# Sliding-window attention with sinks and a highway layer: scores in key halves, with bias and sinks' values issued among them

## The chip, the cores and the metric

The kernel runs on one core of a Trainium2 chip. The metric is device time in microseconds (us) of one execution, the median of several runs; lower is better. The core has a matrix engine (TensorE, called PE in the profile; its weight loads are the row PEld), a vector engine (VectorE, DVE), a scalar engine (ScalarE, ACT), a general engine (GpSimd, POOL) and SyncE (SP), which here only issues DMAs. TensorE writes its results to PSUM, which ACT and DVE read.

## The reference

Four batches, eight heads, 768 positions, head size 64. Each query sees the four first keys (the sinks) and the 128 newest keys up to itself. The result goes through a highway layer of width 512.

```python
keep = is_sink | in_window          # pos < 4, or 0 <= query - key < 128
scores = np.where(keep, scale * q @ k.T, -1e9)
a = softmax(scores)
x = (a @ v)                         # to (3072, 512), the heads side by side
H = np.maximum(x @ w_h, 0.0)
T = 1.0 / (1.0 + np.exp(-(x @ w_t + b_t)))
return T * H + (1.0 - T) * x
```

## The kernel before

The 4 x 768 positions are cut into N = 24 blocks of 128, six to a batch (block n is block c = n % 6 of batch n // 6). The loop runs over n from 0 to 25 as a pipeline: in turn n the kernel makes the scores of the keys of block n, the attention values of block n-1 (n1) and the highway layer of block n-2 (nb). The order of the instructions on each engine is that in which the code issues them; `_keep_traced_order` forbids any other.

**Scores (L264 to L283).** The keys of block n are seen by the queries of blocks n and n+1, 256 queries in all (128 in the last block of a batch). Keys stand on the 128 output rows, queries on the columns. Heads lie in four groups of 32 partitions (g = 0 to 3, two heads hg in each, and the 64 numbers of a head in two halves e), so every product contracts over 32 partitions and uses one of four row groups of the matrix array. The masks come first: for each x (own queries, next block's queries) and g one matmul of 32 rows, 128 columns of weights and 256 moving columns (L271) adds a very negative number where the key isn't in the window. Then 16 matmuls of the same shape add the scores (L278). `expo` (L326, ACT) takes the exponential of all of it out of PSUM.

**Starts (L304 to L318).** Between the scores and the values stand the first products of two accumulations, in the same 32-row shape: the bias of the gate (L310, one matmul of 512 columns into `ps_z`) and the sinks' share of the values (L316, two matmuls of 260 columns into `ps_av`, both in row group j = t-2, with t the block's place in its batch; the first two blocks of a batch have none). The bias stands in another row group than the sinks.

**Values and the highway layer.** 16 matmuls of 128 x 128 weights and 65 columns (8 in a batch's first block) make the values of block n-1 (L337, L340). DVE divides by the sums (`norm`, L348, L350). PE multiplies block n-2 with `wt` (`gate`, L370, four of 512 columns) and the first half with `wh` (`hidden`, L389), transposes block n-1 (L361, four of 128 columns), and does the second half of `hidden`. ACT takes tanh out of `ps_z` (L377) and copies the transposed block (L366). DVE and POOL finish the block (`diff`, `gated`, `finish`), and SP stores it. Once per batch (twice in the first) PE makes the scores of the sinks for up to four tiles (L292, weights of 128 rows by 32 columns, 64 moving columns).

**Loads.** q and k are loaded by POOL (L108, only block 0's and part of the next rows' queries by SP and ACT), v, the sinks' values (`load_sinks`, L171, four DMAs a batch) and the stores are on SP's queue. DVE transposes q and k in tiles of 32 x 32 (L124). POOL casts v (L141).

Of the kernel before, what the change touches and what calls it, by code (L numbers as in the profile page):

```python
# [37 lines left out]
def kernel(  # L38
# [35 lines left out]
    const = ctx.enter_context(tc.tile_pool(name="const", bufs=1))  # L74
# [21 lines left out]
    tr = [data.tile([P, 2, HG, S, 2], FP16, tag=f"tr{b}", name=f"tr{b}")  # L96
          for b in range(B)]
# [42 lines left out]
    def cast_v(n, engine):  # L140
# [5 lines left out]
    away = const.tile([P, P], FP32, tag="away")  # L146
    powers = const.tile([P, 4, P], FP32, tag="powers")
    inside = const.tile([P, P], FP32, tag="inside")
    mq = const.tile([P, 2, P], BF16, tag="mq")
    mk = const.tile([P, 2, P], BF16, tag="mk")  # L150
    mk_0 = const.tile([P, 2, P], BF16, tag="mk_0")
# [7 lines left out]
    skmask = const.tile([P, HG, H], FP16, tag="skmask")  # L159
    vs = [const.tile([P, H, D + 1], FP16, tag=f"vs{b}", name=f"vs{b}") for b in range(B)]  # L160
    sk = [const.tile([P, HG, 2, H, NSINK], FP16, tag=f"sk{b}", name=f"sk{b}")
          for b in range(B)]
# [14 lines left out]
    pool.iota(away, pattern=[[1, P]], base=0, channel_multiplier=-4,  # L177
              allow_small_or_imprecise_dtypes=True)
# [17 lines left out]

    dve.memset(ebias, _EXP_BIAS)
    for g in range(1, G):
        m = away[32 * g:32 * g + 32, :]
        dve.tensor_scalar(out=m, in0=m, scalar1=float(P * g), scalar2=None, op0=ALU.add)  # L200

    dve.tensor_scalar(out=powers[:, 0], in0=away, scalar1=1.0, scalar2=0.0,
                      op0=ALU.add, op1=ALU.max)
# [12 lines left out]
    act.activation(out=powers, in_=powers, func=AF.Exp, scale=_STEEP)  # L218
    dve.tensor_copy(out=mq, in_=powers[:, 0:2])
    dve.tensor_tensor(out=mk, in0=powers[:, 2:4],  # L220
                      in1=inside.unsqueeze(1).to_broadcast([P, 2, P]), op=ALU.mult)
    dve.tensor_copy(out=mk_0, in_=mk)
    dve.memset(mk_0[:, :, 0:NSINK], 0.0)

    dve.memset(ones, 0.0)

# [10 lines left out]
                       func=AF.Copy, bias=1.0)  # L237

    def sink_masks():
        dve.memset(skmask, 0.0)  # L240
        for g in range(G):
            for hg in range(HG):
                h = hg * G + g
                dve.memset(skmask[32 * g:32 * g + 32, hg, h:h + 1], 1.0)
        dve.tensor_scalar(out=below, in0=vmask, scalar1=float(NSINK - 1), scalar2=None,
                          op0=ALU.is_le)
        dve.scalar_tensor_tensor(out=vmask, in0=vmask, scalar=0.0, in1=below,
                                 op0=ALU.is_ge, op1=ALU.mult)

    def sink_keys(b, engine=pool):  # L250
        for hg in range(HG):
            engine.tensor_tensor(
                out=sk[b][:, hg],
                in0=tr[b][:, 1, hg, 0:NSINK, :].rearrange("p s e -> p e s").unsqueeze(2)
                .to_broadcast([P, 2, H, NSINK]),
                in1=skmask[:, hg].unsqueeze(1).unsqueeze(3)
                .to_broadcast([P, 2, H, NSINK]), op=ALU.mult)
# [6 lines left out]
    def scores(n):  # L264
        b, c = divmod(n, NC)
        nq = 2 if c + 1 < NC else 1
        keys = mk_0 if c == 0 else mk
        for x in range(nq):
            for g in range(G):
                rows = slice(32 * g, 32 * g + 32)  # L270
                pe.matmul(ps_s[:, g, :, x * P:(x + 1) * P], lhsT=keys[rows, x],  # L271
                          rhs=mq[rows, x].unsqueeze(1).to_broadcast([32, HG, P]),
                          start=(x == 0), stop=False, skip_group_check=True)
        for hg in range(HG):
            for e in range(2):
                for g in range(G):
                    rows = slice(32 * g, 32 * g + 32)
                    last = pe.matmul(ps_s[:, g, hg, 0:nq * P],  # L278
                                     lhsT=tr[b][rows, 1, hg, c * P:(c + 1) * P, e],
                                     rhs=tr[b][rows, 0, hg, c * P:(c + nq) * P, e],  # L280
                                     start=False, stop=(e == 1),
                                     skip_group_check=True)
        return last  # L283

    def sink_scores(b, tiles):
        for half in range(2):
            for hg in range(HG):
                for e in range(2):
                    for t in tiles:
                        j = t - 2  # L290
                        q0 = t * P + 64 * half
                        pe.matmul(ps_av[32 * j:32 * j + 32, half, SINKS:SINKS + 64],  # L292
                                  lhsT=sk[b][:, hg, e].rearrange("p h s -> p (h s)"),
                                  rhs=tr[b][:, 0, hg, q0:q0 + 64, e],
                                  start=(hg == 0 and e == 0), stop=(hg == HG - 1 and e == 1),
                                  skip_group_check=True)

    def sink_expo(b, tiles):
        rows = slice(32 * (tiles[0] - 2), 32 * (tiles[-1] - 1))
# [1 line left out]
                       in_=ps_av[rows, :, SINKS:SINKS + 64],  # L301
                       func=AF.Exp, bias=ebias[rows], scale=SCALE)

    def starts(n1, n0):  # L304

        j = n1 % NC - 2 if n1 is not None else -1
        if n0 is not None:
            g = (j + 2) % G
            rows = slice(32 * g, 32 * g + 32)
            pe.matmul(ps_z, lhsT=ones[rows], rhs=brow[rows], start=True, stop=False,  # L310
                      skip_group_check=True)
        if j >= 0:
            b = n1 // NC
            rows = slice(32 * j, 32 * j + 32)
            for hg in range(HG):
                pe.matmul(ps_av[:, hg, 0:AV], lhsT=es[b % 2][rows],  # L316
                          rhs=vs[b][rows, G * hg:G * hg + G, :].rearrange("p h e -> p (h e)"),
                          start=True, stop=False, skip_group_check=True)  # L318

    E = [None] * N  # L320

# [123 lines left out]
    for b in range(1, B):  # L445
# [126 lines left out]
    last = N - 1  # L572
# [43 lines left out]
```

## Time and profile before

| | |
|---|---|
| median of 3 runs | 112.94 us (112.66 to 113.4) |
| the profiled execution | 112.83 us, of which the span is 110.9 us |
| mean granted TensorE clock | 0.973 |
| PE busy | 98.7 us (89%), 1414 matmuls |
| DVE busy | 86.1 us (78%) |
| POOL busy | 83.4 us (75%) |
| ACT busy | 76.6 us (69%) |
| 16 DMA engines | 20.81 MB in 36704 packets |

The span is what the profile covers; the execution's own time is 1.9 us longer. Matmul times in it reach from the start to a modelled end, so matmuls that follow each other overlap in the rows: the step from start to start is what one costs. Four matmuls in four row groups start together, and then the rows show a wave of four at one place. "PEld ... <-issue" is a weight load that began late though nothing that the profile shows held it.

### The profile page before, as it was taken

The numbers are of one execution on the slowest core, as the hardware profiler recorded it, in microseconds if no ns is written. First come the engines' busy times: TensorE is split into PE (matmuls) and PEld (weight loads), VectorE is DVE, ScalarE is ACT, GpSimd is POOL, SyncE is SP. The second block draws the span as 40 slices with busy tenths as digits, with TensorE's granted clock in tenths as the row PEclk, the third lists the DMA queues.
The fourth block names the chain that finished last, engine by engine and source line by source line (L and its number), as shares of the span: only waits on it lengthen the run. The fifth ranks groups of instructions, "written<-read, shape, count | busy, mean of one in ns | idle before, by whom it ended". The sixth has DMA issues, their size and how long they took to land.

```text
span 110.9 us, 3573 instructions
## 1 busy us (share of the span) xinstructions
PE 98.7 (89%) x1414; PEld 52.0 (47%) x1414; DVE 86.1 (78%) x186; ACT 76.6 (69%) x96; POOL 83.4 (75%) x136
## 2 busy tenths in 40 slices
PE   5996698669997999999999999999999999999900
PEld 2332354424553455556545455565645565544500
DVE  6776745475599669869988997889889969987980
ACT  4487738567837477879849786987679877974700
POOL 6897529919896999997999999996477629886000
PEclk9999859999999999999999999999999999999995
DMA  3999999999999499999999999999984672242422
GB/s 95 213 222 211 178 204 204 152 174 228 173 229 191 95 197 308 210 204 232 212 200 244 261 231 178 216 238 168 253 236 109 184 185 105 111 173 97 193 95 95
DMA packets 36704, 20.81 MB, mean 188 GB/s; under 512 B 27340, under 2 KB 33232, under 8 KB 36688
## 3 DMA queue, kind: packets, MB, share of 16 engines
q1 hardware_dynamic: 29536, 13.37, 45.5%
q0 software_dynamic: 6848, 6.82, 40.1%
q10 hardware_dynamic: 304, 0.39, 1.2%
q8 instruction: 11, 0.18, 0.7%
q14 instruction: 5, 0.04, 0.1%
HBM read 21.11 MB, written 6.29 MB: 247 GB/s over the span
## 4 chain that ended last, share of the span: by engine, by line
PE 38%; DMA 28%; POOL 13%; DVE 10%; issue 5%; ACT 2%; DVEq 0%; POOLq 0%; ACTq 0%
PE ps_h L389 9%; PE ps_z L370 9%; DMA nat<-in_k_dram 8%; DMA wt<-in_moe_w_t_dram 8%; DMA wh<-in_moe_w_h_dram 7%; POOL nat L108 6%; DMA nat<-in_q_dram 5%; PE ps_s L278 4%; PE ps_av L361 3%; PE ps_s L271 3%; PE ps_av L337 3%; PE ps_av L340 3%; POOL O L413 3%; DVE DD L402 2%; PE ps_z L310 2%
## 5 line engine op out<-in xcount | busy, mean ns | idle before, releaser
L326 ACT ACTIVATE E<-ps_s,ebias 128x2048 f16<-128x2048 f32 (+1 forms) x24 | 43.8, 1825 | 14.3 <-PE ps_s L278 14.3
L413 POOL TENSOR_TENSOR O<-DD,X 128x512 f32<-128x512 f16 x19 | 21.9, 1156 | 10.1 <-issue 7.0
L108 POOL DMA_DIRECT2D nat<-in_k_dram x40 | 21.8, 550 | 7.5 <-DMA wt<-in_moe_w_t_dram 2.7
L389 PE MATMUL ps_h<-wh,XT 128*128 128x512 f16 (+1 forms) x96 | 27.4, 375 | 0.0
L124 DVE STREAM_TRANSPOSE tr<-nat 128x384 f32<-128x384 f32 (+1 forms) x28 | 26.1, 961 | 0.9 <-DMA nat<-in_q_dram 0.7
L370 PE MATMUL ps_z<-wt,XT 128*128 128x512 f16 x96 | 24.6, 379 | 0.0
L402 DVE SCALAR_TENSOR_TENSOR DD<-ps_h,X 128x512 f16<-128x512 f32 (+1 forms) x24 | 16.1, 671 | 6.2 <-PE ps_h L389 6.2
L377 ACT ACTIVATE TH<-ps_z 128x512 f16<-128x512 f32 x24 | 14.2, 591 | 6.7 <-PE ps_z L370 6.7
L108 POOL DMA_DIRECT2D nat<-in_q_dram x32 | 17.6, 557 | 0.6 <-DMA nat<-in_k_dram 0.5
L350 DVE TENSOR_TENSOR X<-ps_av,rec 128x512 f16<-128x512 f32 x24 | 16.6, 691 | 0.8
L366 ACT COPY XT<-ps_av 128x512 f16<-128x512 f16 x24 | 14.1, 586 | 4.5 <-PE ps_av L361 2.7
L278 PE MATMUL ps_s<-tr 32*128 32x256 f16 (+1 forms) x384 | 14.6, 267 | 2.1 <-DVE tr L124 2.1
L340 PE MATMUL ps_av<-v,E 128*128 128x65 f16 x192 | 14.1, 193 | 1.7 <-DVE v L141 0.8
L340 PEld LDWEIGHTS <-E 128*128 128x128 f16 x192 | 11.8, 97 | 2.2 <-issue 2.2
L337 PEld LDWEIGHTS <-E 128*128 128x128 f16 x160 | 10.2, 97 | 5.7 <-issue 5.7
L337 PE MATMUL ps_av<-v,E 128*128 128x65 f16 x160 | 12.7, 194 | 0.0
L141 POOL CAST v<-V 128x512 f16<-128x512 f32 x19 | 12.6, 661 | 0.0
L389 PEld LDWEIGHTS <-XT 128*128 128x128 f16 x100 | 8.7, 98 | 6.7 <-issue 0.4
L348 DVE RECIPROCAL rec<-ps_av 128x8 f32<-128x8 f32 x24 | 4.9, 204 | 8.3 <-PE ps_av L340 7.9
L278 PEld LDWEIGHTS <-tr 32*128 32x128 f16 x384 | 9.3, 94 | 4.4 <-DVE tr L124 2.1
L361 PEld LDWEIGHTS <-X 128*128 128x128 f16 x96 | 5.9, 99 | 10.0 <-DVE X L350 10.0
L361 PE MATMUL ps_av<-ident,X 128*128 128x128 f16 x96 | 9.6, 224 | 1.1 <-DVE X L350 0.9
(64 smaller groups left out, 105.9 us busy)
## 6 DMA issues: line engine op xcount, KB each, us to landing
V<-in_v_dram SPq DMA_DIRECT2D x24, 256.0 KB, 5.4
out_dram<-O SPq DMA_DIRECT2D x23, 256.0 KB, 2.7
nat<-in_k_dram POOLq DMA_DIRECT2D x24, 64.0 KB, 4.1
nat<-in_q_dram POOLq DMA_DIRECT2D x16, 96.0 KB, 4.6
nat<-in_k_dram POOLq DMA_DIRECT2D x16, 96.0 KB, 4.5
nat<-in_q_dram POOLq DMA_DIRECT2D x16, 64.0 KB, 5.3
first<-in_q_dram SPq DMA_DIRECT2D x6, 128.0 KB, 4.0
wt<-in_moe_w_t_dram POOLq DMA_DIRECT2D x1, 512.0 KB, 8.5
```

The lines of the kernel that those rows point to most:

```text
L108: engine.dma_start(out=into[32 * g:32 * g + 32].rearrange("p hg m d -> p hg (m d)"), in_=(q, k)[which][b, :, t0:t0 + nt, :].rearrange("(hg ...
L124: dve.transpose(out=dst, in_=src)
L278: last = pe.matmul(ps_s[:, g, hg, 0:nq * P], lhsT=tr[b][rows, 1, hg, c * P:(c + 1) * P, e], rhs=tr[b][rows, 0, hg, c * P:(c + nq) * P, e], ...
L326: act.activation(out=E[n][:, :, :, 0:nq * P], in_=ps_s[:, :, :, 0:nq * P], func=AF.Exp, bias=ebias, scale=SCALE)
L337: pe.matmul(slot, lhsT=E[n - 1][:, g, hg, P:2 * P], rhs=v_of(n - 1)[:, h, :], start=first, stop=False, skip_group_check=True)
L340: pe.matmul(slot, lhsT=E[n][:, g, hg, 0:P], rhs=v_of(n)[:, h, :], start=first, stop=True, skip_group_check=True)
L350: dve.tensor_tensor(out=X[n], in0=av[:, :, :, 0:D], in1=rec.unsqueeze(3).to_broadcast([P, HG, G, D]), op=ALU.mult)
L361: pe.transpose(xt[:, kc // 2, (kc % 2) * P:(kc % 2 + 1) * P], x[:, kc * P:(kc + 1) * P], ident)
L370: pe.matmul(ps_z, lhsT=XT[n][:, kc * P:(kc + 1) * P], rhs=wt[:, kc, :], start=False, stop=(kc == KC - 1), skip_group_check=True)
L389: pe.matmul(into, lhsT=XT[n][:, kc * P:(kc + 1) * P], rhs=wh[:, kc, cols], start=(kc == 0), stop=(kc == KC - 1), skip_group_check=True)
L402: dve.scalar_tensor_tensor(out=DD[n][:, cols], in0=ps_h[:, cols] if h is None else h, scalar=0.0, in1=flat(X[n], cols), op0=ALU.max, op1=A ...
L413: eng.tensor_tensor(out=O[n][:, cols], in0=DD[n][:, cols], in1=flat(X[n], cols), op=ALU.add)
```

## The change

The scores of a block are made in two halves of 64 keys each, so the weights are 32 rows by 64 columns and a row group holds two of them, one for the output rows 0 to 63 and one for 64 to 127. A half's products run only over the 192 queries that can see it (256 in a batch's first block). The two masks become one product per half and group (256 columns for the two diagonal squares); the squares that are wholly outside are written only in a batch's first two blocks and then stay in PSUM. A block has 8 mask matmuls and 32 score matmuls of this shape instead of 8 and 16 of 32 x 128. In a batch's first two blocks four more matmuls of 128 columns write the outside squares (eight more in block 0).

In blocks 7 to 23 the starts no longer follow the scores but stand among them: the bias as two matmuls of 256 columns, one after the first quarter of the scores and one after the third, and the sinks' values after the last score. The bias stays in one row group ("first": 0 or 2); the sinks' two matmuls go to two row groups, one each. For this the sinks' keys and values lie differently: `sk` has a zero quarter on each side of the keys, `load_sinks` takes eight DMAs a batch instead of four, the es rows are shared out by head half. The constants of the masks are made for 64 keys, with a few small vector operations more.

```diff
     def load_sinks(b, gs=range(G)):
         for g in gs:
-            sp.dma_start(out=vs32[32 * g:32 * g + 32, b, 0:D], in_=v[b, :, 0:NSINK, :])
+            hs = slice(G * (g % 2), G * (g % 2) + G)
+            for r0 in (32 * g, 32 * g + 16):
+                sp.dma_start(out=vs32[r0:r0 + 16, b, 0:D], in_=v[b, hs, 0:NSINK, :])
...
+    def masks(n):
+        c = n % NC
+        nq = 2 if c + 1 < NC else 1
+        for half in range(2):
+            ks = slice(K2 * half, K2 * half + K2)
+            keys = mk_0 if c == 0 and half == 0 else mk
+            for g in range(G):
+                rows = slice(32 * g, 32 * g + 32)
+                at = ps_s[ks, g].rearrange("p hg (x f) -> p hg x f", x=2)
+                pe.matmul(at[:, :, 0:nq, ks], lhsT=keys[rows],
+                          rhs=mq[rows, 0:nq].unsqueeze(1).to_broadcast([32, HG, nq, K2]),
+                          start=True, stop=False, skip_group_check=True)
...
+    def products(n, u, g):
+
         b, c = divmod(n, NC)
         nq = 2 if c + 1 < NC else 1
...
+        hg, e = divmod(u, 2)
+        rows = slice(32 * g, 32 * g + 32)
+        for half in range(2):
+            ks = slice(K2 * half, K2 * half + K2)
+            q0 = K2 * half
+            q1 = min(nq * P, 2 * P if half or c == 0 else 3 * K2)
+            k0 = c * P + K2 * half
+            last = pe.matmul(ps_s[ks, g, hg, q0:q1],
+                             lhsT=tr[b][rows, 1, hg, k0:k0 + K2, e],
+                             rhs=tr[b][rows, 0, hg, c * P + q0:c * P + q1, e],
+                             start=False, stop=(e == 1), skip_group_check=True)
+        return last
...
+    def bias(g, half):
+        rows = slice(32 * g, 32 * g + 32)
+        cols = slice(half * DM // 2, (half + 1) * DM // 2)
+        pe.matmul(ps_z[:, cols], lhsT=ones[rows], rhs=brow[rows, cols], start=(half == 0),
+                  stop=False, skip_group_check=True)
+
+    def sinks(n1, hg):
+        b, t = divmod(n1, NC)
+        i, odd = divmod(t - 2, 2)
+        rows = slice(32 * (2 * i + hg), 32 * (2 * i + hg) + 32)
+        pe.matmul(ps_av[:, hg, 0:AV], lhsT=es[b % 2][rows],
+                  rhs=vs[b][rows, G * odd:G * odd + G, :].rearrange("p h e -> p (h e)"),
+                  start=True, stop=False, skip_group_check=True)
...
+    def scores_and_starts(n):
+        n1 = n - 1
+        t = n1 % NC
+        first = 0 if t >= 4 else 2
+        others = [g for g in range(G) if g != first]
+        masks(n)
+        for g in range(G):
+            products(n, 0, g)
+        bias(first, 0)
+        for u in (1, 2):
+            for g in others:
+                products(n, u, g)
+            if u == 1:
+                products(n, 1, first)
+        bias(first, 1)
+        for g in others:
+            products(n, 3, g)
+        for u in (2, 3):
+            last = products(n, u, first)
+        if t >= 2:
+            for hg in range(HG):
+                sinks(n1, hg)
+        return last
...
+        joined = 7 <= n < N
         if n < N:
-            after = scores(n)
+            after = scores_and_starts(n) if joined else scores(n)
...
-        starts(n1 if 0 <= n1 < N else None, nb if nb >= 0 else None)
+        if not joined:
+            starts(n1 if 0 <= n1 < N else None, nb if nb >= 0 else None)
```

In blocks 0 to 6 the scores are made in halves too (`masks`, then all `products`), and the starts follow them as before.

More of the change, by code (lines that the diff above doesn't have):

```diff
@@ L145 @@
     zeros = const.tile([P, DM], FP16, tag="zeros")
[L146 to L151, printed above, removed]
+    K2 = P // 2
+    away = const.tile([P, K2], FP32, tag="away")
+    row = const.tile([P, 1], FP32, tag="row")
+    part = const.tile([P, 2], FP32, tag="part")
+    powers = const.tile([P, 4, K2], FP32, tag="powers")
+    inside = const.tile([P, K2], FP32, tag="inside")
+    mq = const.tile([P, 2, K2], BF16, tag="mq")
+    mq_out = const.tile([P, 2, K2], BF16, tag="mq_out")
+    mk = const.tile([P, K2], BF16, tag="mk")
+    mk_0 = const.tile([P, K2], BF16, tag="mk_0")
     wh = const.tile([P, KC, DM], FP16, tag="wh")
@@ L218 @@
     act.activation(out=powers, in_=powers, func=AF.Exp, scale=_STEEP)
[L219 to L221 removed]
+    for x in range(2):
+        dve.tensor_scalar(out=mq[:, x], in0=powers[:, x], scalar1=part[:, x:x + 1], scalar2=None,
+                          op0=ALU.mult)
+        dve.tensor_copy(out=mq_out[:, x], in_=part[:, x:x + 1].to_broadcast([P, K2]))
+        dve.tensor_scalar(out=powers[:, 2 + x], in0=powers[:, 2 + x], scalar1=part[:, x:x + 1],
+                          scalar2=None, op0=ALU.mult)
+    dve.tensor_tensor(out=powers[:, 2], in0=powers[:, 2], in1=powers[:, 3], op=ALU.add)
+    dve.tensor_tensor(out=mk, in0=powers[:, 2], in1=inside, op=ALU.mult)
     dve.tensor_copy(out=mk_0, in_=mk)
[L223 removed]
+    dve.memset(mk_0[:, 0:NSINK], 0.0)
     dve.memset(ones, 0.0)
@@ L262, in sink_values @@
             in1=vmask.unsqueeze(2).to_broadcast([P, H, D + 1]), op=ALU.mult)
-    def scores(n):
+    def masks(n):
[11 more added lines that the diff above has]
+        for half in range(2):
+            if c < 2 if half == 0 else n == 0:
+                ks = slice(K2 * half, K2 * half + K2)
+                keys = mk_0 if c == 0 and half == 0 else mk
+                for g in range(G):
+                    rows = slice(32 * g, 32 * g + 32)
+                    at = ps_s[ks, g].rearrange("p hg (x f) -> p hg x f", x=2)
+                    pe.matmul(at[:, :, 1 - half, K2 - K2 * half:P - K2 * half], lhsT=keys[rows],
+                              rhs=mq_out[rows, 1 - half].unsqueeze(1).to_broadcast([32, HG, K2]),
+                              start=False, stop=False, skip_group_check=True)
@@ L265, in scores @@
+    def products(n, u, g):
         b, c = divmod(n, NC)
         nq = 2 if c + 1 < NC else 1
-        keys = mk_0 if c == 0 else mk
-        for x in range(nq):
-            for g in range(G):
[L270 to L282, printed above, removed]
+        hg, e = divmod(u, 2)
+        rows = slice(32 * g, 32 * g + 32)
+        for half in range(2):
+            ks = slice(K2 * half, K2 * half + K2)
+            q0 = K2 * half
[6 more added lines that the diff above has]
+        return last
@@ L283, in scores @@
+    def scores(n):
+        masks(n)
+        for u in range(4):
+            for g in range(G):
+                last = products(n, u, g)
         return last
@@ L286, in sink_scores @@
         for half in range(2):
-            for hg in range(HG):
+            for odd in range(2):
                 for e in range(2):
[L289 to L296, printed above, removed]
+                    for i in range(tiles[0] // 2 - 1, tiles[-1] // 2):
+                        q0 = (2 * i + 2 + odd) * P + 64 * half
+                        for hg in range(HG):
+                            r0 = 32 * (2 * i + hg)
+                            pe.matmul(ps_av[r0:r0 + 32, half, SINKS:SINKS + 64],
+                                      lhsT=sk[:, b, hg, e].rearrange("p x g s -> p (x g s)")[
+                                          :, 16 - 16 * odd:48 - 16 * odd],
+                                      rhs=tr[b][:, 0, hg, q0:q0 + 64, e],
+                                      start=(odd == 0 and e == 0), stop=(odd == 1 and e == 1),
+                                      skip_group_check=True)
     def sink_expo(b, tiles):
@@ L302, in sink_expo @@
                        func=AF.Exp, bias=ebias[rows], scale=SCALE)
+    def bias(g, half):
+        rows = slice(32 * g, 32 * g + 32)
+        cols = slice(half * DM // 2, (half + 1) * DM // 2)
[8 more added lines that the diff above has]
+                  start=True, stop=False, skip_group_check=True)
     def starts(n1, n0):
-        j = n1 % NC - 2 if n1 is not None else -1
         if n0 is not None:
[L308 to L314, printed above, removed]
-            for hg in range(HG):
-                pe.matmul(ps_av[:, hg, 0:AV], lhsT=es[b % 2][rows],
-                          rhs=vs[b][rows, G * hg:G * hg + G, :].rearrange("p h e -> p (h e)"),
-                          start=True, stop=False, skip_group_check=True)
+            for half in range(2):
+                bias(3 if n1 is not None and n1 % NC in (2, 3) else 1, half)
+        if n1 is not None and n1 % NC >= 2:
+            for hg in range(HG):
+                sinks(n1, hg)
[4 more added lines that the diff above has]
+        others = [g for g in range(G) if g != first]
+        masks(n)
+        for g in range(G):
+            products(n, 0, g)
[11 more added lines that the diff above has]
+        if t >= 2:
+            for hg in range(HG):
+                sinks(n1, hg)
+        return last
     E = [None] * N
```

28 lines of the change are left out of this document (17 added, 11 removed).

## The prediction

> **What bounds the kernel now.** First the stretches, to see which engine is full where; then the waits; then PE's own rows inside one block. The columns of the stretches are length, busy time of PE, PEld, DVE, ACT and POOL (with the number of instructions), granted clock, DMA share and GB/s.
>
> ```profile
> 0.00:38.80 38.80, 32.46 (x388) 15.33 (x389) 26.11 (x69) 23.94 (x36) 29.70 (x61) 0.96 1.03 183
> 38.80:56.00 17.20, 16.93 (x286) 9.58 (x285) 14.34 (x28) 13.73 (x16) 16.27 (x26) 1.00 1.04 226
> 56.00:97.00 41.00, 40.85 (x670) 22.91 (x669) 36.42 (x72) 33.41 (x38) 33.48 (x47) 1.00 0.85 194
> 97.00:111.00 14.00, 8.43 (x87) 4.15 (x74) 9.24 (x20) 5.52 (x9) 3.99 (x5) 0.91 0.35 131
> ```
>
> Blocks 7 to 23 begin at 38.80, 42.43, 46.45, ... 93.07 and 96.61 us (starts of their first mask, L271). From block 7 on PE is full: 57.8 of 58.2 us up to 97. DVE has 36.4 of 41 there, so it is near, but not the limit. Before 38.8 PE waits for loads. In 38.8 to 97 PE's rows leave only five real holes, 0.42 us at 40.1 for a cast of v and 0.04, 0.26, 0.20 and 0.19 us at 52.9, 56.3, 66.9 and 77.9 for X (L350). So what is added to PE in blocks 7 to 23 lengthens the kernel, less some 1.1 us of holes that it fills.
>
> PE's time isn't all streaming. The waits have a wait of weight loads for nothing visible, in every block, at the first mask and at the first value:
>
> ```profile
> PEld L271 <- issue: 9.1, 21, 0.9
> PEld L337 <- issue: 5.7, 21, 0.7
> ```
>
> PE's rows in block 16 (first fence) and at the sinks' scores of block 14 (second) show what lies there:
>
> ```profile
> 71.39 0.38 PE L389 MATMUL ps_h<-wh,XT 128*128 128x512 f16 x1
> 71.70 0.40 PE L271 MATMUL ps_s<-mq,mk 32*128 32x256 bf16 x8
> 71.93 0.28 PE L278 MATMUL ps_s<-tr 32*128 32x256 f16 x4
> 72.39 0.27 PE L316 MATMUL ps_av<-vs,es 32*128 32x260 f16 x1
> 72.39 0.37 PE L310 MATMUL ps_z<-brow,ones 32*128 32x512 f16 x1
> 72.50 0.27 PE L316 MATMUL ps_av<-vs,es 32*128 32x260 f16 x1
> 72.70 0.20 PE L337 MATMUL ps_av<-v,E 128*128 128x65 f16 x1
> ```
>
> ```profile
> 66.94 0.40 PE L361 MATMUL ps_av<-ident,X 128*128 128x128 f16 x4
> 67.26 0.21 PE L292 MATMUL ps_av<-tr,sk 128*32 128x64 f16 x4
> 67.30 0.39 PE L292 MATMUL ps_av<-tr,sk 128*32 128x64 f16 x28
> 67.63 0.39 PE L389 MATMUL ps_h<-wh,XT 128*128 128x512 f16 x1
> ```
>
> ```profile
> 71.11 0.22 PE ps_av L361 x4
> 73.36 0.86 PE ps_z L370 x4
> ```
>
> The last two lines are of the chain: 512 columns take 0.215 us and 128 take 0.055, 0.42 ns a column. The last L389 of 71.39 has thus streamed its columns by 71.605, yet the first mask starts at 71.70: 0.095 us in which nothing streams. The last sinks' matmul (72.50, 260 columns, 0.11) is through by 72.61; the first value starts at 72.70: 0.09. Transposes (128 x 128) to sinks' scores (128 rows, 32 columns): through by 67.165, next start 67.26, again 0.095; and the way back costs 0.098. Wherever the shape of the weight tile changes, be it in rows or in columns, PE stands 0.092 to 0.099 us, at nearly all such places after 20 us; between matmuls of one shape the step is the streaming time and 0.002. Inside one shape, tiles at different places of the array run side by side: four row groups start within 0.01 us and the next four 0.11 later (256 columns), and four column tiles of L292 start within 0.01 and the next four 0.03 later.
>
> **The change part by part.**
>
> *Scores themselves.* Eight tiles of 32 x 64 side by side are in no trace here, but four rows and four columns each are. I take eight side by side, with 0.0035 us between starts (0.025 for eight) and the row's small step: a mask wave 0.119 (the first wave of L271 has that), a product of 192 columns 0.081, 0.085 to the next. Alone that is one mask wave and four of products, 0.48 us, instead of six waves, 0.69 us: a saving of 0.2 us a block. Bounds: 0.2 saved; or, if halves take turns, 0.107 + 4 x 0.085 = 0.45 more than this.
>
> *Shape changes.* A block before has two: into 32 x 128 at the masks, out of it at the values. After, bias (L360) and sinks (L367) are still 32 x 128 while masks and scores are 32 x 64. A joined block goes 128x128, 32x64, bias, 32x64, bias, 32x64, sinks, 128x128: seven changes, six where there are no sinks. A change between 32 x 64 and 32 x 128 is in no trace of before. The lower bound is 0; the upper, all tiles end, then 0.095. I take 0.095, since all four kinds that are shown cost it, among them one in which only the columns change.
>
> The Trainium skill, TensorEngine Tiling (Array Packing), Key Properties, says that changing the tiling mode, not just the tile, drains TensorE, and lists 32 x 64 and 32 x 128 as two modes. By that rule each of the five added changes is paid, as in the sum below; if only the change of rows counted, as one could also read the rows of L271 and L316, the sum would be that of the first rival.
>
> *A joined block's sum*, from first mask to first value. Masks and first quarter: 0.119 + 0.025 + 0.081 = 0.225. Change, bias of 256 columns alone, change: 0.095 + 0.107 + 0.095 = 0.297. Second and third quarter: 0.085 + 0.018 + 0.081 = 0.184. Change, bias, change: 0.297. The last products, where the bias's own row group has two to make up: 0.021 + 0.085 + 0.004 + 0.081 = 0.191. Change, sinks side by side, change: 0.095 + 0.113 + 0.095 = 0.303. Together 1.497 us; before, 71.70 to 72.70, 0.999: +0.50. For the kinds of block:
> - c = 3 or 4 (n = 9, 10, 15, 16, 21, 22): 6 x 0.50 = 2.99.
> - c = 2, no sinks (8, 14, 20): 1.289 against 0.993: 3 x 0.30 = 0.89.
> - c = 1, no sinks, four outside squares of 128 columns more (0.055): 7, 13, 19: 3 x 0.35 = 1.05.
> - c = 0, outside squares, and 256 columns in the upper half (12, 18): 2 x 0.67 = 1.34.
> - c = 5, 128 queries (11, 17, 23): about 1.31 against 0.70: 3 x 0.61 = 1.83.
>
> Sum +8.1 us. Off it go the holes that this fills: X's 0.69 us, 0.35 of the cast's 0.42 (block 7 is delayed by that much). At the end E of block 23 starts at 97.38 behind ACT's tanh and gate value, some 0.2 us after its scores, and the division of block 22 (98.51) comes about 0.5 us after its values end, so some 0.45 us of block 23's delay isn't seen. That leaves 8.1 - 1.5 = +6.6 us.
>
> *What is late next.* The exponential starts after the last product, now 1.19 us after the first mask instead of 0.69. E (1.97 us) then ends 3.44 and tanh 3.93 after it, with a block of 4.04 us. The bias moves ahead, to 0.32 after the next first mask, 4.36: it waits for tanh's read of `ps_z`, with 0.4 us to spare (0.8 before). DVE and POOL get slack.
>
> *Weight loads.* 40 loads of 64 columns instead of 24 of 128. L292's 32 loads of 32 columns keep to 0.03 us for four; 64 columns at that pace fit under 0.06, a product lasts 0.081. I take 0; if the two loads of a row group came one after the other at 0.06, a product's step would be 0.12 instead of 0.085, 17 x 4 x 0.035 = +2.4 us, the upper bound. The Trainium skill, TensorEngine Tiling (Array Packing), Restrictions, says that column tiling switches the fast weight load off. That rule speaks for the upper bound, 121.8 us in all; L292, a column tile too, keeps its pace here.
>
> *Blocks 0 to 6, loads, constants.* Blocks 0 to 6 save 0.2 us of scores and pay one change: -0.1 each, but PE waits there for tiles and casts (1.32 us at 20.4, 0.78 at 24.3, 0.45 at 33.7, 0.73 at 36.3), so 0. On SP's queue two sinks' DMAs more stand ahead of the second rows of q (`first`), whose cast (9.18) waits for them. The rows have 0.78 us an issue early, 0.68 later, so up to 1.56 us late in block 1. V's loads follow the scores, so this passes on some blocks; the holes at 33.7 and 36.3, 1.2 us, are waits for loads and POOL that don't move with PE. I take 0, bound +1.5. Later, four more issues a batch (2.7 us) stand between V's loads, three blocks ahead, and stores: 0. DVE's constants become more and smaller operations (3.8 us before, about as much after) and a memset of `sk` (0.4) replaces small ones: 0, bound 0.3. The starts of turn 24: -0.1 at best, left out.
>
> **Sum.** The profiled execution's 112.83 us (0.11 under the median) + 6.6 = 119.4 us.
>
> **Rivals.**
> 1. *The change between 32 x 64 and 32 x 128 is free* and bias and sinks do run in free row groups. The fullest row group then has 0.119 + 4 x 0.085 + 2 x 0.109 = 0.68, sinks end at 0.71, values start at 0.80 instead of 1.00: -0.2 in 9 blocks, -0.15 in three, about -0.03 in five, -2.4 in all. DVE (89% busy) gives back some 0.3: 110.7 us. For it: no row shows this change. Against: 128 x 32 after 128 x 128 costs 0.095 though rows stay.
> 2. *Only the row group that changes waits.* Others go on, but matmuls start in order. Bias starts at 0.315, the second quarter's part in its group at 0.517, the second bias at 0.693, its last products at 0.895 and 0.98, sinks until 1.10, values at 1.19: +0.19 (0.16 without sinks, more for c = 0 and 5), 3.9 in all, less 1.3: 115.4 us. For it: row groups start independently within a shape. Against: nothing tells it from a full stop.
> 3. *The halves don't run side by side*, so the change doesn't do what it says: 17 x 0.45 = 7.6 more than the forecast, 127 us. Against: L292.
>
> **How the numbers follow.** Forecast (full stop at each change) 0.77: 117.5 to 122, since five stops of 0.092 to 0.099 are narrow, but the overlap within quarters and the filled holes may be 1 us wrong each, and SP's delay or the weight loads may add 1 or 2. Rival 1 0.14, rival 2 0.07, rival 3 0.02. A range of 113 to 122 holds rival 2 and nearly all of the forecast, some 0.82; what it leaves out is rivals 1 and 3. About 1% (1.1 us) can be told from no change. Faster 0.13; same 0.06 (rival 1 with SP's delay passed on, or a mild rival 2); slower 0.81.
>
> **What would show it.** Right: in joined blocks, holes of 0.09 to 0.1 us on both sides of each bias (L360) and before the sinks; first mask to first value 1.4 to 1.6 us; blocks of 4.0 us; waits of weight loads "issue" at L323 and L360 that did not exist; no more waits for X. Rival 1: bias rows that start within 0.01 us of products, 0.8 us to the first value. Rival 2: other groups' products starting right after the bias. Rival 3: products of the two halves 0.08 us apart. Wrong altogether: PE idle for DVE or ACT in 56 to 97 us.

## The result and the profile after

The changed kernel takes 123.99 us in the median (123.39 to 124.6), the kernel before 113.17 us in the same comparison: ratio 1.0957, 95% interval 1.0881 to 1.1033, slower. (Ratios here and below are of undisturbed executions alone, so they are not the ratios of the medians.) The profiled execution took 123.94 us, its span is 121.7 us. Forecast were 119.4 us and 113 to 122: the direction was right, the loss was put at 6.6 us and is 10.8 (11.1 between the two profiled executions).

The stretches, cut at the first mask of block 7 and of block 23; first the kernel after, then the one line of the kernel before that was not shown above (columns as above).

```profile
0.00:41.57 41.57, 32.07 (x524) 15.80 (x524) 27.71 (x78) 23.74 (x36) 32.20 (x66) 0.92 1.04 184
41.57:107.11 65.54, 65.54 (x1233) 33.74 (x1232) 50.68 (x98) 46.73 (x52) 46.21 (x69) 1.00 0.77 175
107.11:122.00 14.89, 9.20 (x119) 4.84 (x118) 9.75 (x20) 6.02 (x10) 3.33 (x4) 0.93 0.32 118
```

```profile
38.80:96.61 57.81, 57.39 (x933) 32.10 (x933) 50.40 (x98) 46.75 (x52) 49.36 (x72) 1.00 0.91 205
```

The sixteen blocks 7 to 22 take 65.54 us instead of 57.81, +7.73. Blocks 0 to 6 take 41.57 instead of 38.80, +2.77. What follows the first mask of block 23 takes 14.60 of the span instead of 14.33. DVE and ACT do the same work in the middle stretch, POOL three instructions less; PE alone is full. 933 matmuls have become 1233, yet that isn't what fills it. PE's rows of block 10 show what does:

```profile
53.66 0.38 PE L474 MATMUL ps_h<-wh,XT 128*128 128x512 f16 x1
53.97 0.32 PE L298 MATMUL ps_s<-mq,mk 32*64 32x256 bf16 x8
54.10 0.27 PE L323 MATMUL ps_s<-tr 32*64 32x192 f16 x8
54.30 0.28 PE L360 MATMUL ps_z<-brow,ones 32*128 32x256 f16 x1
54.51 0.37 PE L323 MATMUL ps_s<-tr 32*64 32x192 f16 x14
54.81 0.28 PE L360 MATMUL ps_z<-brow,ones 32*128 32x256 f16 x1
55.02 0.38 PE L323 MATMUL ps_s<-tr 32*64 32x192 f16 x10
55.33 0.28 PE L367 MATMUL ps_av<-vs,es 32*128 32x260 f16 x2
55.55 0.20 PE L422 MATMUL ps_av<-v,E 128*128 128x65 f16 x1
```

The eight products at 54.10 all start within 0.024 us, so the last has streamed its 192 columns (0.08 us, at 0.42 ns a column) by 54.21. The bias starts at 54.30, and nothing runs beside it: its 256 columns are through by 54.41, the next products start at 54.51. The same at 54.81 and 55.02, and before 55.33 and 55.55. Each change of the weight tile between 32 x 64 and 32 x 128 is a full stop of 0.092 to 0.105 us: no matmul of any row group starts in it. First mask to first value is 1.58 us instead of 1.00. The trace agrees here with the Trainium skill, TensorEngine Tiling (Array Packing), Key Properties, by which changing the tiling mode drains TensorE: a change of the tile's columns alone, with 32 rows kept, is a change of mode.

### The profile page after: what moved, and what is told of

Same layout as the page of the kernel before. It is cut to its first block, busy times and chain, and to the rows that moved or that the text cites. A ratio compares the mean times of both kernels' runs of the same rounds, so it can differ in the third digit from the quotient of the medians.

```text
span 121.7 us, 4522 instructions
## 1 busy us (share of the span) xinstructions
PE 106.8 (88%) x1874; PEld 54.4 (45%) x1874; DVE 88.1 (72%) x195; ACT 76.5 (63%) x96; POOL 81.7 (67%) x137
## 3 DMA queue, kind: packets, MB, share of 16 engines
HBM read 21.11 MB, written 6.29 MB: 225 GB/s over the span
## 4 chain that ended last, share of the span: by engine, by line
PE 62%; DMA 13%; SPq 8%; DVE 5%; POOL 5%; issue 4%; DVEq 0%; POOLq 0%
PE ps_h L474 14%; PE ps_z L455 13%; PE ps_s L323 10%; DMA nat<-in_q_dram 8%; PE ps_z L360 6%; SPq L178 5%; DMA vs<-in_v_dram 5%; PE ps_av L422 5%; PE ps_av L425 4%; POOL nat L108 4%; PE ps_av L446 3%; PE ps_s L298 3%; PE ps_av L367 2%; SPq L108 2%; DVE tr L124 1%
## 5 line engine op out<-in xcount | busy, mean ns | idle before, releaser
L323 PE MATMUL ps_s<-tr 32*64 32x192 f16 (+3 forms) x768 | 21.4, 253 | 5.5 <-DVE tr L124 5.5
L455 PE MATMUL ps_z<-wt,XT 128*128 128x512 f16 x96 | 25.2, 386 | 0.0
L425 PE MATMUL ps_av<-v,E 128*128 128x65 f16 x192 | 14.7, 198 | 1.2 <-DVE v L141 1.2
L323 PEld LDWEIGHTS <-tr 32*64 32x64 f16 x768 | 10.7, 105 | 11.0 <-DVE tr L124 5.2
L425 PEld LDWEIGHTS <-E 128*128 128x128 f16 x192 | 12.2, 100 | 1.8 <-issue 1.3
L422 PE MATMUL ps_av<-v,E 128*128 128x65 f16 x160 | 12.9, 197 | 0.0
L360 PE MATMUL ps_z<-brow,ones 32*128 32x256 f16 x48 | 12.3, 281 | 0.0
L422 PEld LDWEIGHTS <-E 128*128 128x128 f16 x160 | 10.5, 99 | 3.2 <-issue 1.6
L141 POOL CAST v<-V 128x512 f16<-128x512 f32 x19 | 11.6, 612 | 0.0
L474 PEld LDWEIGHTS <-XT 128*128 128x128 f16 x100 | 8.6, 98 | 6.5 <-issue 0.2
L455 PEld LDWEIGHTS <-XT 128*128 128x128 f16 x96 | 7.9, 100 | 6.2 <-issue 0.6
```

The source lines that it names most:

```text
L323: last = pe.matmul(ps_s[ks, g, hg, q0:q1], lhsT=tr[b][rows, 1, hg, k0:k0 + K2, e], rhs=tr[b][rows, 0, hg, c * P + q0:c * P + q1, e], start ...
L360: pe.matmul(ps_z[:, cols], lhsT=ones[rows], rhs=brow[rows, cols], start=(half == 0), stop=False, skip_group_check=True)
L422: pe.matmul(slot, lhsT=E[n - 1][:, g, hg, P:2 * P], rhs=v_of(n - 1)[:, h, :], start=first, stop=False, skip_group_check=True)
L425: pe.matmul(slot, lhsT=E[n][:, g, hg, 0:P], rhs=v_of(n)[:, h, :], start=first, stop=True, skip_group_check=True)
L455: pe.matmul(ps_z, lhsT=XT[n][:, kc * P:(kc + 1) * P], rhs=wt[:, kc, :], start=False, stop=(kc == KC - 1), skip_group_check=True)
L474: pe.matmul(into, lhsT=XT[n][:, kc * P:(kc + 1) * P], rhs=wh[:, kc, cols], start=(kc == 0), stop=(kc == KC - 1), skip_group_check=True)
```

## The experiments

One table first; the stretch "7 to 22" is from the first mask of block 7 to that of block 23, "12 to 22" is its later part, which in nearly all these runs is free of waits on loads. The columns on blocks are of the one profiled execution.

| kernel | median us | ratio to before (95%) | block 6 begins | block 7 begins | 7 to 22 | 12 to 22 |
|---|---|---|---|---|---|---|
| before, the profile shown | 113.17 | | 33.0 | 38.80 | 57.81 | 39.52 |
| before_again | 112.21, one execution | | 31.9 | 38.22 | 57.72 | 39.5 |
| the change, the profile shown | 123.99 | 1.0957 (1.0881 to 1.1033) | 36.5 | 41.57 | 65.54 | 45.13 |
| change_again | 123.75, one execution | | 36.3 | 41.38 | 65.54 | 45.1 |
| bias_at_one_place | 119.65 | 1.0537 (1.0432 to 1.0641) | 36.9 | 41.96 | 60.64 | 41.7 |
| halves_alone | 114.93 | 1.011 (1.0053 to 1.0167) | 35.4 | 40.51 | 57.33 | 39.3 |
| one_shape | 114.79 | 1.0015 (0.9917 to 1.0113) | 35.5 | 40.78 | 60.23 | 39.1 |
| one_shape_filled | 114.11 | 1.0051 (1.0008 to 1.0094) | 33.0 | 40.35 | 58.02 | 39.2 |
| one_shape_tuned | 117.14 | 1.0375 (1.0241 to 1.051) | 34.5 | 41.64 | 58.16 | 39.9 |
| sinks_loads_doubled | 114.42 | 1.007 (1.0023 to 1.0117) | 35.1 | 40.41 | 57.52 | 39.5 |
| change_old_loads | 123.88 | 1.0927 (1.088 to 1.0975) | 33.5 | 40.46 | 66.68 | 45.9 |
| change_filled | 123.68 | 1.0925 (1.0858 to 1.0993) | 36.0 | 41.11 | 65.56 | 45.1 |
| change_loads_moved | 122.06 | 1.0863 (1.073 to 1.0997) | 33.6 | 39.49 | 65.56 | 45.1 |
| before_filled | 112.91 | 0.9978 (0.9938 to 1.0019) | 33.0 | 40.41 | 57.52 | 39.5 |

Before's own median in these comparisons was 113.37 to 113.54 us. The profiled execution was not always a typical one: those of one_shape (117.38 us), one_shape_filled (114.9) and before_filled (114.2) are each the longest of ten.

**Two stops fewer (bias_at_one_place).**

```diff
         bias(first, 0)
+        bias(first, 1)
         for u in (1, 2):
...
-        bias(first, 1)
         for g in others:
             products(n, 3, g)
```

> The changed kernel with both halves of the bias behind the first quarter of the scores, so two shape changes fewer in each of the blocks 7 to 23 and the same matmuls. Theory (each shape change is a full stop): 2 x 0.1 and the longer first wave, 0.23 us a block, 17 x 0.23 = 3.9 us less than the changed kernel: 120 us. Rival (bias matmuls among the scores cost their own time alone, stops or not): 123.5 to 124.5 us.

119.65 us, and blocks 7 to 22 in 60.64 us, 4.90 less than the change with the very same matmuls. Block 10's rows:

```profile
53.44 0.32 PE L298 MATMUL ps_s<-mq,mk 32*64 32x256 bf16 x8
53.57 0.27 PE L323 MATMUL ps_s<-tr 32*64 32x192 f16 x8
53.77 0.39 PE L360 MATMUL ps_z<-brow,ones 32*128 32x256 f16 x2
54.09 0.47 PE L323 MATMUL ps_s<-tr 32*64 32x192 f16 x24
54.49 0.28 PE L367 MATMUL ps_av<-vs,es 32*128 32x260 f16 x2
54.70 0.20 PE L422 MATMUL ps_av<-v,E 128*128 128x65 f16 x1
```

First mask to first value is 1.263 us instead of 1.577, so -0.31 where -0.23 was expected: two stops of 0.1, a slow first wave less, and quarters that now run into each other. The theory holds, the rival falls. Since only the order of the matmuls differs, this run gives the price of a stop with all that hangs on it: (45.13 - 41.74) / 22 = 0.154 us in blocks 12 to 22.

**No stop inside (one_shape).** Scores as in the change, but bias and sinks as two matmuls of 32 x 64 where one of 32 x 128 was; sinks' layout and loads as before.

```diff
+        for ks in (slice(0, K2), slice(K2, P)):
+            pe.matmul(ps_z[ks, cols], lhsT=ones[rows, ks], rhs=brow[rows, cols],
+                      start=(half == 0), stop=False, skip_group_check=True)
...
+        for ks in (slice(0, K2), slice(K2, P)):
+            pe.matmul(ps_av[ks, hg, 0:AV], lhsT=es[b % 2][rows, ks],
```

> Scores in halves, and bias and sinks' values among them in blocks 7 to 23, but these too as tiles of 32 rows by 64 columns (two matmuls where one was), so that no shape changes inside a block's scores; sinks' layout and loads as before. Theory (the shape changes and SP's loads are all of the loss): the fullest row group has 0.134 + 4 x 0.088 + 2 x 0.11 = 0.71 us, first mask to first value 0.82 to 0.85 instead of 1.00, so -2.5 to -3 us, of which waits for X give back up to 1: 110 to 112 us, faster than before. Rival (bias and sinks among the scores cost time in themselves, because matmuls start in order): 1.2 us or more to the first value, 116 us or more.

114.79 us, ratio 1.0015 (0.9917 to 1.0113): the loss is gone to about 1%, but there is no gain; neither range is met. In block 16 some of PE's rows are

```profile
76.36 0.32 PE L292 MATMUL ps_s<-mq,mk 32*64 32x256 bf16 x8
76.49 0.34 PE L317 MATMUL ps_s<-tr 32*64 32x192 f16 x11
76.59 0.27 PE L369 MATMUL ps_z<-brow,ones 32*64 32x256 f16 x1
77.22 0.20 PE L422 MATMUL ps_av<-v,E 128*128 128x65 f16 x1
```

The bias (L369) now starts among running products, and the values come 0.86 us after the first mask. So bias and sinks among the scores cost nothing in themselves, and matmuls in free row groups do run side by side as long as the shape stays. In blocks 12 to 22 this is 39.1 us against 39.52, though first mask to first value is 0.94 us less in their sum (0.09 a block). Part of that is taken back: in the filled run of this kernel the holes ahead of the transposes, where PE waits for X, add up to 1.1 us between 56 and 99 us, against 0.65 between 56 and 97 before. X comes from DVE, 89% busy, as the first rival of the prediction has it. In block 9 of this execution PE also stood 1.96 us because the first sinks' matmul of a batch waited for POOL's product (L279) with scores in line behind it, and the clock was halved from 51.6 to 55.1 us; that is why "7 to 22" reads 60.23.

**The halves alone (halves_alone).** The kernel before with `masks` and `products` of the change, their constants, and nothing else.

> The kernel before with the scores in halves of 64 keys and the masks in one product, and nothing else: starts, sinks' layout and loads as before. Theory (a full stop at each change of the weight tile's shape, eight tiles side by side, and a first wave after a stop that is 0.03 us longer): a block has three shape changes instead of two; first mask to first value 0.134 + 0.48 + 0.095 + 0.22 = 0.93 us instead of 1.00, so -0.07 in each of 17 blocks: 111 to 112.5 us. Rival (the halves themselves are what is slow, by their weight loads): a wave of products of 0.11 us instead of 0.088, first mask to first value 1.02 or more, 113 us or more.

114.93 us, ratio 1.011 (1.0053 to 1.0167), a small loss: neither. First mask to first value is 0.92 us in blocks of c = 3 and 4, as the theory has it, but 0.82 instead of 0.72 at c = 5 and 1.07 instead of 1.01 at c = 0, and blocks 12 to 22 take 39.3 us, 0.2 less than before. The loss lies earlier: block 7 began at 40.51; in this execution PE stood 2.47 us in block 3 and the granted clock was half from 20.7 to 27.5 us. Behind that hole is v: DVE stood 1.84 us for a tile of it at 19.93 (0.80 in the profile of before, at 18.89), with the transpose that block 3 needs next in line. Whether halves make such holes likelier is open.

**SP's loads alone (sinks_loads_doubled).** The kernel before, each sinks' load in two of 16 rows.

```diff
-            sp.dma_start(out=vs32[32 * g:32 * g + 32, b, 0:D], in_=v[b, :, 0:NSINK, :])
+            for x in range(2):
+                r0 = 32 * g + 16 * x
+                sp.dma_start(out=vs32[r0:r0 + 16, b, 0:D],
+                             in_=v[b, G * x:G * x + G, 0:NSINK, :])
```

> The kernel before with each of the four sinks' loads of a batch cut into two of 16 rows, as many DMAs on SP's queue as in the change and nothing else changed. Theory (the early loss of the change, 2.8 us before block 7, is SP's queue): block 7 begins 1.5 to 3 us later than at 38.8, 114.5 to 116 us. Rival (the delay is filled by holes that wait for loads, as the prediction had it, and the early loss of the change comes from the scores in blocks 0 to 6): block 7 at 38.8 to 39.3 us, 113 us.

114.42 us, ratio 1.007 (1.0023 to 1.0117): a loss clear of noise, just under the range of the theory. Blocks 6 and 7 begin 2.1 and 1.6 us later than in the profile of before. These two starts don't show the loads' share by themselves: the granted clock was half from 12.8 to 23.0 us in this execution, against 12.8 to 16.2 in before's, and before_filled, with the loads of before, begins block 7 at 40.41 as well.

**The change with SP's loads elsewhere (change_loads_moved).** The same eight loads a batch, behind what is needed first.

```diff
-    load_sinks(0, range(2))
...
-    load_sinks(0, range(2, G))
+    load_sinks(0)
...
-            if n % NC == 3 and n // NC + 1 < B:
+            if n % NC == 4 and n // NC + 1 < B:
```

> The changed kernel with its eight sinks' loads a batch at other places of SP's queue: batch 0's behind the second rows of q and the first two tiles of v instead of ahead of them, the later batches' one turn later, behind that turn's v. Theory (the early loss is what waits behind these loads: q's second rows and v): block 6 begins at 33 to 34.5 us instead of 36.5, and block 7 at 39 to 40.5 instead of 41.6; blocks 7 to 23 take 65.5 us as in the change; 122 to 123 us. Rival (the early loss is the other early work of the change, its masks' constants and the memset of sk): block 6 at 36 us or later, 123.5 to 124.5 us.

122.06 us (121.77 to 122.85), 1.9 less than the change. Block 6 begins at 33.6 instead of 36.5, block 7 at 39.49 instead of 41.57, and the sixteen blocks take 65.56, as they did. The theory holds for the loads taken together; the run moves both groups at once, those of batch 0 and those of the later batches. SP's queue in the change, then in the kernel before (start, duration, what; some rows left out):

```profile
1.63 2.83 SPq L178 DMA_DIRECT2D vs<-in_v_dram  x4
4.50 1.85 SPq L108 DMA_DIRECT2D first<-in_q_dram  x4
6.39 1.44 SPq L131 DMA_DIRECT2D V<-in_v_dram  x2
7.88 4.38 SPq L178 DMA_DIRECT2D vs<-in_v_dram  x4
22.39 7.73 SPq L178 DMA_DIRECT2D vs<-in_v_dram  x8
30.21 3.44 SPq L131 DMA_DIRECT2D V<-in_v_dram  x3
```

```profile
1.64 1.56 SPq L173 DMA_DIRECT2D vs<-in_v_dram  x2
3.24 1.96 SPq L108 DMA_DIRECT2D first<-in_q_dram  x4
5.24 1.06 SPq L131 DMA_DIRECT2D V<-in_v_dram  x2
21.47 2.88 SPq L173 DMA_DIRECT2D vs<-in_v_dram  x4
24.93 5.26 SPq L131 DMA_DIRECT2D V<-in_v_dram  x3
```

A load of half the rows takes nearly as long to issue (mostly 0.63 us instead of 0.68), so eight cost nearly twice four. q's second rows go out 1.26 us later. Behind the next four loads v's third tile goes out at 12.38 instead of 9.29. Before block 5 the queue is held for 7.7 us, and the next v goes out at 30.2 instead of 24.9; but no row shows anything waiting for that tile: POOL casts it at 35.51 us, in the kernel before at 35.63.

**Old loads under the change (change_old_loads).** Sinks' layout and loads as before, all seven shape changes kept, the sinks' two matmuls one after the other.

> The changed kernel with the sinks' layout and the four loads a batch of before; bias and sinks stand among the scores in 32 x 128 as in the change, but both sinks' matmuls in one row group, one after the other (0.11 us more in 11 blocks, 1.2 us). Theory (the early loss is mostly SP's eight loads): block 7 begins at 39 to 40 us instead of 41.6, the 16 blocks after it take 66.5 us instead of 65.5, 122.5 to 123.5 us in all. Rival (the early loss comes from the half clock after PE's long holes in blocks 3 and 4, whoever makes the holes): block 7 at 40.5 us or later when the granted clock shows one or two halved windows there, as in the run with the halves alone.

123.88 us. Block 6 begins at 33.5 and the sixteen blocks take 66.68, both as expected, but block 7 begins only at 40.46 and the time misses its range. The rival isn't the reason: the one halved window of the clock (22.0 to 25.4) was past by block 6. Between 33.5 and 40.46 two DVE operations took 1.26 us each (0.27 and 0.43 in before) while POOL worked, and PE stood 1.26 us for DVE's result at 38.85. before_filled shows the same more plainly.

**Filled holes (change_filled, before_filled).** Matmuls on zeros where PE waits for a transposed tile.

> The changed kernel with matmuls on zeros (128 x 128 weights, 512 columns, 0.215 us each, into ps_h, not used yet) between masks and scores of block 3 (one) and block 4 (eight), where PE waits 0.56 and 2.4 us for the transposed tile. Theory (part of the early loss is the halved clock that the hole of block 4 brings, 27.8 to 31.2 us in the changed kernel's profile): no halved window there, block 7 begins 1 to 1.7 us earlier, at 40 to 40.6, 122.3 to 123 us. Rival (the hole alone is the loss, the clock falls on work that waits anyway): block 7 at 41.3 to 41.8 us, 124 us.

> The kernel before with matmuls on zeros where PE waits for the transposed tile: four in block 3 (hole of 1.3 us), two in block 4 (0.78 us). Theory (the halved clock after such holes is what spreads the executions and costs up to 1.7 us when it comes): 112 to 113 us, 0 to 1 us less than before, by as much as before has such windows in part of its executions. Rival (no part of the time hangs on it): 113 to 113.6 us.

In the change no halved window follows block 4 any more, yet block 7 begins at 41.11, only 0.3 to 0.5 us earlier, and 123.68 us isn't told apart from the change. The rival's number is nearer, but the run doesn't show its reason: from block 4 to block 5 this execution took 6.29 us instead of 7.84, and it had lost 1.07 us before block 4, where DVE stood 1.76 us for a tile of v. In the kernel before, 112.91 us isn't told apart from no change; but in the profiled execution block 7 began at 40.41 after a block 6 at 33.0, where the profile shown has 33.0 and 38.80. DVE and POOL in block 6, first in that run, then in the profile of before (some rows left out):

```profile
33.86 0.66 POOL L141 CAST v<-V 128x512 f16<-128x512 f32 x1
34.10 1.69 DVE L384 TENSOR_SCALAR TH<-TH 128x512 f16<-128x512 f16 x1
34.44 1.19 POOL L414 TENSOR_TENSOR O<-DD,X 128x512 f32<-128x512 f16 x1
```

```profile
34.06 0.27 DVE L383 TENSOR_SCALAR TH<-TH 128x512 f16<-128x512 f16 x1
34.71 0.29 DVE L383 TENSOR_SCALAR TH<-TH 128x512 f16<-128x512 f16 x1
35.63 0.62 POOL L141 CAST v<-V 128x512 f16<-128x512 f32 x1
```

One DVE operation takes 1.69 us instead of 0.27 while POOL works, and it ends 0.16 us after POOL's second one. PE then stands 1.72 us for DVE's result (38.81). The Trainium skill, SBUF — State Buffer, Who interferes with whom, names DVE's `tensor_scalar` in a two-port mode and GpSimd as takers of one exclusive lock; these rows agree. It is a matter of which work meets: both executions reach block 6 at 33.0, but in the profile of before POOL had stood 0.95 us for a load, and its cast came at 35.63, behind these operations. The four executions with the longest such operations in block 6 (1.26 to 1.69 us) begin block 7 between 6.96 and 7.39 us after block 6, the others after 5.1 to 6.3; the change, 3 us late, doesn't meet it (0.27 and 0.29).

**The unchanged kernels again (before_again, change_again).**

> The kernel before, unchanged, one more profile. Theory (blocks 0 to 6 differ between executions, by where the granted clock halves and by whether DVE's work of block 6 falls on POOL's, which made one DVE operation 1.69 us instead of 0.29 in the filled kernel): block 7 begins at 38.8 to 40.5 us, blocks 7 to 23 take 57.5 to 57.8 us. Rival (the profile shown is the rule): block 7 at 38.7 to 38.9 us.

> The changed kernel, unchanged, one more profile. Theory: blocks 7 to 23 take 65.5 us again to 0.1 us, block 7 begins at 41 to 42 us.

The sixteen blocks repeat to 0.1 us, 57.72 and 65.54. Block 7 began at 41.38 in the change, as expected, and at 38.22 in the kernel before, earlier than either range. The profile of before is no exception then, but the filled and the halved kernels show 40.4 and 40.5 with the same loads: a single start of block 7 is good to 1 or 2 us only. Block 6 is steadier. With the eight loads where the change has them it began at 35.1 to 36.9 us in five executions; with the loads of before, or moved, at 31.9 to 33.6 in six, and at 34.5 to 35.5 in three (halves_alone, one_shape, one_shape_tuned).

**One shape without holes (one_shape_filled, one_shape_tuned).**

> As the run with one shape (scores, bias and sinks all in tiles of 32 x 64, loads as before), with the sinks' matmuls behind the last score, so that a late share of the sinks holds up no score, and six matmuls on zeros where PE waits 2.06 us for the transposed tile in block 3. Theory: blocks 7 to 23 in 56.3 to 57 us instead of 57.8 (first mask to first value 0.85 to 0.95), block 7 at 39 to 40 us without a halved clock: 111 to 112.5 us, at or a little under before. Rival (PE's saving goes into waits for X and DVE, which is 89% busy): 57.5 us or more, 113 us or more.

> As the filled run with one shape, with the first two sinks' loads behind the first tiles of v and the sinks' values made one turn earlier on POOL, so that the first sinks' matmul of a batch, which held PE for 0.98 us in block 9, doesn't wait. Theory: no hole in block 9, blocks 7 to 23 in 56.5 to 57 us, 112 to 113.3 us, equal to before or up to 1% faster. Rival (POOL is full there, so earlier values only push its other work back): 57.5 us or more, 113.5 to 114.5 us.

114.11 us, ratio 1.0051 (1.0008 to 1.0094), and 117.14 us, ratio 1.0375 (1.0241 to 1.051). Both miss. In the first, block 7 waits for DVE and POOL as above (40.35) and block 9 still 0.98 us for POOL's product. In the second that hole is 0.40, but block 7 begins at 41.64 and PE waits 0.60 for X at 66.4. No version here beats the kernel before.

## Why the prediction was right or wrong

- *Each change of shape is a full stop*: right, shown by the gaps at every bias of the joined blocks and by dose. Blocks 12 to 22 take 45.1 us with seven or six changes a block, 41.7 with two fewer, 39.3 with three (halves alone), 39.1 with two. Only the first two of these differ in nothing else.
- *Eight tiles side by side*: right. The eight products of a wave start within 0.024 us; rival 3 fell. Rivals 1 and 2 fell with the gaps: no product of another row group starts before the bias is through.
- *The joined block's sum* and *weight loads at 0*: mis-sized. 1.577 us measured against 1.497 in block 10, and 0.06 to 0.09 too little in each kind (more in blocks 7 and 8). The term is the first wave after a stop. Masks to first products took 0.134 us where 0.119 was put in, products to products 0.112 twice where 0.085 was put in; the last 0.01 us is in the stops. In a block without stops inside (block 3 of the change) the step is 0.087 to 0.090, as assumed. So a stop also costs some 0.03 us behind it, nearly the 0.12 a wave that the upper bound of the weight loads put in. In the trace the weight loads of all 14 products behind a stop begin only after it, from 54.51 on; that this slows the wave is likely, no run isolates it. Over the sixteen blocks the forecast had 6.4 us (6.6 less 0.16 seen of block 23); 7.73 came, 1.3 more.
- *What the added time fills*: right. First mask to first value sums to 24.24 us over the blocks 7 to 22 instead of 15.75, 8.5 more, while the blocks took 7.73 more; with the hole for the cast that the 15.75 hold, some 1 us went into holes.
- *What is late next*: right. PE waits for neither tanh nor the exponential; it is busy for all of the 65.54 us.
- *Blocks 0 to 6 and SP's loads at 0, bound +1.5*: wrong, and the larger error: +2.77. Rows of the change, then of the kernel before:

```profile
10.73 0.69 DVE L566 CAST nat<-first 128x1024 f16<-128x1024 f32 x1 [2.14 <-DMA first<-in_q_dram]
25.24 0.43 DVE L141 CAST v<-V 128x512 f16<-128x512 f32 x1 [1.39 <-DMA V<-in_v_dram]
25.58 1.09 DVE L124 STREAM_TRANSPOSE tr<-nat 128x512 f32<-128x512 f32 x1
37.16 0.66 PE L323 MATMUL ps_s<-tr 32*64 32x256 f16 x32 [0.34 <-DVE tr L124]
```

```profile
9.18 0.69 DVE L481 CAST nat<-first 128x1024 f16<-128x1024 f32 x1 [1.23 <-DMA first<-in_q_dram]
22.77 0.42 DVE L141 CAST v<-V 128x512 f16<-128x512 f32 x1
23.10 1.09 DVE L124 STREAM_TRANSPOSE tr<-nat 128x512 f32<-128x512 f32 x1
33.68 0.63 PE L278 MATMUL ps_s<-tr 32*128 32x256 f16 x16 [0.29 <-DVE tr L124]
36.30 0.19 PE L340 MATMUL ps_av<-v,E 128*128 128x65 f16 x1 [0.56 <-POOL v L141]
```

  Two steps failed. The first is the delay's size. The part that was priced came as priced: the cast of q's second rows starts 1.55 us later. But the delay grew from there. DVE casts v and transposes q and k, one after the other in the order of the code; in the change it stands 1.39 us for a tile of v at 25.24, with the transpose for block 4 behind it, which starts 2.48 us late, and block 6 begins 3.46 us late. That the delay passes on through v's loads was said, but not priced. The second step is that the holes at 33.7 and 36.3 would swallow the delay since they don't move with PE. One did: the hole for POOL's cast is gone, and block 7 is only 2.77 us late. The other didn't: 0.45 us at 33.7 became 0.50 at 37.2, since the tile that PE waits for there is transposed by DVE right behind X of the block before, so it moves along. Moving the loads gave back 1.9 us of the time and 2.9 us at block 6, so they are most of it. Which of the two groups counted stays open, as does why that tile of v, sent 1.73 us later, landed nearly 5 us later. What remains of block 7's delay in that run, 0.7 to 1.3 us, goes with two DVE operations of 1.03 and 0.82 us beside POOL (0.27 and 0.43 undisturbed).
- *The end*: +0.27 us against +0.16.

6.6 + 1.3 + 2.8 + 0.1 (the end) is 10.8, against 11.1 between the profiled executions, of which 0.3 lie outside the span. The direction and the mechanism of the larger part were right; the forecast fell short by the slow first wave and by blocks 0 to 6.

## What to carry to other kernels

Count the changes of the weight tile's shape on PE's path, in rows and in columns alike, and price each at a full stop and a slow first wave (together 0.15 us here); work put "in free row groups" is free only in the shape that runs there. Cutting a small DMA in two nearly doubled its issue on the queue here, and what counts is what stands behind it at that moment, in the filling of the pipeline above all. A hole that a profile shows is cover only if its releaser doesn't hang on the engine that is being delayed. And look at more than one execution before a few tenths in the filling are explained.

## What the runs showed of the hardware

The stop was expected (0.092 to 0.105 us in the change); that the wave behind it is slower was not: 0.112 us instead of 0.087 for 192 columns. A DMA of 16 rows of 256 bytes took 0.63 us to issue on SP's queue, one of 32 rows 0.68. A DVE operation of 0.27 us took up to 1.69 beside POOL (before_filled), and PE stood 1.72 us behind it.
